# Attention over agents and two feed-forward layers on one core: another issue order at block ends, and three scalings and four additions moved to the pool engine

## Chip, core and metric

One core of a Trainium2 chip. TensorE multiplies matrices into PSUM banks, VectorE and ScalarE read the banks and work on SBUF, the pool engine (POOL in the rows) works on SBUF alone, and SyncE issues DMA transfers. Each engine takes its instructions in program order and waits on semaphores. The metric is the device time of one execution in microseconds (us), lower is better. A time is given as the median of several runs; one further execution was recorded by the profiler.

## What is computed

```
q, k, v: 12480 x 128; agents: 49 x 128; scale = 1 / sqrt(128)
agent_v = softmax(scale * agents @ k.T) @ v              # 49 x 128
x  = softmax(scale * q @ agents.T) @ agent_v             # 12480 x 128
x  = relu(x @ w_in1) ** 2 @ w_out1                       # 128 -> 2048 -> 128
h  = x @ w_in2                                           # 128 -> 2048
out = (max(h, 0) + alpha * min(h, 0)) @ w_out2           # 2048 -> 128
```

All arrays are 32-bit floats or wider on the host.

## The kernel before

A first part, to about 119 us, loads `k`, `v` and the weights and computes the small `agent_v`. It folds `agent_v` into `w_in1` (tiles `W1h`, `W1l`). The main loop then works on the 12480 tokens in 25 blocks, the first of 320 tokens, 23 of 512 and the last of 384. All products are made of three matmuls on a high and a low part of each operand (`...h` and `...l`: a rounded copy and what the rounding left), and each runs as a pair on the two halves of 64 partitions. A "pair" in this text is such two matmuls.

The hidden size of 2048 is cut into eight steps per block (`NP = 8`). Step `s = 8b + i` is step i of block b. One turn of the loop issues, for several blocks at once:

- `H1(s)`, 3 pairs: hidden part of the first layer into bank pair h1, then a relu on ScalarE into `g`. `G1(s)` squares `g` on ScalarE, rounds it on VectorE (`g1h`) and subtracts (`g1l`).
- `O(s - 2)`, 6 pairs: the first layer's output, added up over the eight steps in bank pair o1.
- `H2(s - 11)`, 6 pairs: hidden part of the second layer into bank pair h2; relu on ScalarE into `g2h`, then on VectorE `g2l = max(h, 0) - g2h`.
- `O2`, one step behind its H2, 6 pairs: the second layer's output in bank pair o2. In the first step of a block three more pairs add the linear term: the second layer is written as (1 - alpha) relu(h) + alpha h, and alpha h goes through one 128 x 128 matrix `M` (`Mh`, `Ml`).

h1, h2, o1 and o2 have one buffer each, so a bank pair is filled again only after VectorE and ScalarE have read it. Around the block's end:

- In steps with i = 1 the sums of o1 are complete. `X1(b)` copies one bank on ScalarE, adds the other on VectorE (`x`), makes `xh` on ScalarE and `xl` on VectorE, and issues four DMA copies that exchange the halves of the partitions (`sh`, `sl`). The next block's first O comes at i = 2, the first H2 that reads `xh`, `xl`, `sh` and `sl` at i = 3.
- In the same steps `q_scores` computes the attention scores of the next block (matmuls into h1), and `q_squares` transposes them on VectorE (`s`). At i = 4, ahead of H1, `q_max` runs on VectorE (`mx`, `m`, `s`), at i = 5 `q_norm`.
- The last O2 of a block comes at i = 3. `OUT` copies one bank of o2 on ScalarE and adds the other on VectorE (`o`), transposes (`ot`) and stores; it stands at the head of the turn i = 4, behind `q_max`. The next block's first O2 comes at i = 4.

`M` is built in steps 10 to 19: `m_scale(g)` multiplies a quarter of `w_out2` by alpha (steps 10 to 13; g = 2 on the pool engine, the others on VectorE), `m_join(g)` adds `wi2h` and `wi2l` on VectorE at the end of steps 11, 13, 15 and 17, `m_transpose(g)` turns that on TensorE one step later (bank pair h1, tile `wT_ps`), with a ScalarE copy, and `m_finish(g)` multiplies and adds up two steps later. The order of all this is that of the Python text; no scheduler changes it. In early steps some `g1l` run on the pool engine: `LO_ON_POOL = (0, 3, 4, 6, 7, 9, 10, 11, 15)`.

The engines' work of the loop, as it stands in the turn before the change:

```
            if s < S:
                G1(s)
            bx, ix = divmod(s - LAG1, NP)
            if ix == NP - 1 and 0 <= bx < NB:
                X1(bx)
            if 0 <= s - D < S:
                H2(s - D)
                pend.append(s - D)
```

Of the kernel before, what the change touches and what calls it, by code (L numbers as in the profile page):

```python
# [8 lines left out]
F32 = mybir.dt.float32  # L9
# [3 lines left out]
AF = mybir.ActivationFunctionType  # L13
ALU = mybir.AluOpType
# [5 lines left out]
def agent_attention_moe_kernel(  # L20
# [30 lines left out]
    nc = tc.nc  # L51
# [10 lines left out]
    NP = FC // 2  # L62
    SCALE = 1.0 / float(C) ** 0.5
    QB = 32
    NT = 512
# [4 lines left out]
    NB = len(NQS)  # L70
    H = 64
    GA = (NA + 1) // 2
    LAG1, LAG2 = 2, 1
    D = NP + LAG1 + 1
    S = NB * NP
# [16 lines left out]
    def ps(tag, name):  # L92

        return psum.tile([128, 2, NT], F32, tag=tag, name=name)
# [7 lines left out]
    def rows(r):  # L102
        return slice(r * H, (r + 1) * H)

    def mm2(o, terms, start=True, stop=True):

        for n_, term in enumerate(terms):
            for r in range(2):
                mm(o(r), *term(r), start=(start and n_ == 0), stop=(stop and n_ == len(terms) - 1))

    def f32(ap):
        return ap.bitcast(F32)
# [56 lines left out]
    with tc.manual_schedule():  # L169
# [19 lines left out]
        wi2h = const.tile([128, 2, NP, 128], F32R, name="wi2h")  # L189
        wi2l = const.tile([128, 2, NP, 128], F32R, name="wi2l")  # L190
# [35 lines left out]
        def flat(t_):  # L226
            return t_.rearrange("p j c -> p (j c)")
# [34 lines left out]
        def q_scores(b):  # L262
            if b >= NB:
                return

            n = QB * NQS[b] // 2
            p_ = ps("h1", "s2_ps")[:, :, :n]
            qh, ql = qh_sb.pop(b), ql_sb.pop(b)
            mm2(
                lambda r: p_[:, r],  # L270
                [
                    lambda r, a=a, x=x, h=h: (a[rows(r), h], x[rows(r), h * n:(h + 1) * n])
                    for h in range(2) for a, x in ((agTl, qh), (agTh, ql), (agTh, qh))
                ],
            )
            s2_ps[b] = p_
# [107 lines left out]
        mT = {}  # L384

        def m_scale(g):
            shape = [128, 4, C]
            w4 = aw[g].rearrange("p (k c) -> p k c", c=C)
            (nc.gpsimd if g == 2 else nc.vector).tensor_tensor(
                out=w4, in0=w4, in1=alp[:, 4 * g:4 * g + 4].unsqueeze(2).to_broadcast(shape), op=ALU.mult  # L390
            )

# [2 lines left out]
        def m_join(g):  # L395
            sl = slice(2 * g, 2 * g + 2)
            mT[g] = stg.tile([128, 2, 2, 128], F32, tag="wf", name="wf", bufs=3)
            nc.vector.tensor_tensor(out=mT[g], in0=f32(wi2h[:, :, sl]), in1=f32(wi2l[:, :, sl]), op=ALU.add)

        def m_transpose(g):  # L400
            w = mT[g]
# [26 lines left out]
        with tc.tile_pool(name="att", bufs=1) as att:  # L428
# [191 lines left out]
            for g in range(2):  # L620
                sl = slice(g * NP // 2, (g + 1) * NP // 2)
                p_ = ps(("h1", "h2")[g], "w1_ps")[:, 0].rearrange("p (i m) -> p i m", m=128)
# [7 lines left out]
        xp = ctx.enter_context(tc.tile_pool(name="xp", bufs=2))  # L630

        h1g, h2g, x1, o1p, o2p, outp = {}, {}, {}, {}, {}, {}

        def width(b):
            return QB * NQS[b]

        def H1(s):
            b, i = divmod(s, NP)
            n = width(b)
            p_ = ps("h1", "h1_ps")[:, :, :n]  # L640
            qh, ql = qs_sb[b]
            mm2(
                lambda r: p_[:, r],
                [lambda r, w=w, x=x: (w[rows(r), i], x[rows(r)]) for w, x in ((W1l, qh), (W1h, ql), (W1h, qh))],
            )
            g = wk.tile([128, 2, NT], F32, tag="g1", name="g1")[:, :, :n]
            nc.scalar.activation(g, p_, AF.Relu)  # L647
            h1g[s] = g

        def G1(s):  # L650
            n = width(s // NP)
            g = h1g.pop(s)
            nc.scalar.activation(g, g, AF.Square)  # L653
            gh = wk.tile([128, 2, NT], F32R, tag="g1h", name="g1h", bufs=3)[:, :, :n]
            gl = wk.tile([128, 2, NT], F32R, tag="g1l", name="g1l", bufs=3)[:, :, :n]
            if s in HI_ON_SCALAR:
                nc.scalar.copy(gh, g)  # L657
            else:
                nc.vector.tensor_copy(gh, g)  # L659
            eng = nc.gpsimd if s in LO_ON_POOL else nc.vector  # L660
            eng.tensor_tensor(out=gl, in0=g, in1=f32(gh), op=ALU.subtract)  # L661
            h1g[s] = (gh, gl)

        def O(s, gs, wh, wl, acc, tag):
            b, i = divmod(s, NP)
            if i == 0:
                acc[b] = ps(tag, tag)[:, :, :width(b)]
            p_ = acc[b]
            terms, last = [], []
            if tag == "o2" and i == (NP - 1 if b == 0 else 0):  # L670
                (xh, _), (xl, _) = x1[b]
                (last if b == 0 else terms).extend([lambda r, m=m, x=x: (m[rows(r)], x[rows(r)]) for m, x in ((Ml, xh), (Mh, xl), (Mh, xh))])
            gh, gl = gs.pop(s)
            for j in range(2):
                terms += [
                    lambda r, w=w, g=g, j=j: (w[rows(r), 2 * i + j], g[rows(r), j])
                    for w, g in ((wl, gh), (wh, gl), (wh, gh))
                ]
            mm2(lambda r: p_[:, r], terms + last, start=(i == 0), stop=(i == NP - 1))

        def X1(b):

            p_ = o1p.pop(b)
            n = width(b)
            x = xp.tile([128, NT], F32, tag="x", name="x", bufs=1)[:, :n]
            nc.scalar.copy(x, p_[:, 0])
            nc.vector.tensor_tensor(out=x, in0=x, in1=p_[:, 1], op=ALU.add)  # L687
            xh, sh, xl, sl = (xp.tile([128, NT], F32R, tag=t, name=t)[:, :n] for t in ("xh", "sh", "xl", "sl"))
            nc.scalar.copy(xh, x)  # L689
            nc.vector.tensor_tensor(out=xl, in0=x, in1=f32(xh), op=ALU.subtract)  # L690
            for a, o in ((xh, sh), (xl, sl)):
                for r in range(2):
                    nc.sync.dma_start(out=f32(o[rows(r)]), in_=f32(a[rows(1 - r)]))
            x1[b] = (xh, sh), (xl, sl)
# [19 lines left out]
        def O2(s):  # L714
            O(s, h2g, wo2h, wo2l, o2p, "o2")
            b, i = divmod(s, NP)
            if i == NP - 1:
                x1.pop(b)
                outp[b] = o2p.pop(b)

        def OUT(b):
            p_ = outp.pop(b)
            x = xp.tile([128, NT], F32, tag="o", name="o", bufs=1)[:, :width(b)]
            nc.scalar.copy(x, p_[:, 0])
            nc.vector.tensor_tensor(out=x, in0=x, in1=p_[:, 1], op=ALU.add)  # L725
            ot = xp.tile([128, NT // QB, QB], F32, tag="ot", name="ot")[:, :NQS[b]]
            nc.vector.transpose(flat(ot), x)
            for i in range(C // QB):
                nc.sync.dma_start(out=ov[i][:, Q0[b]:Q0[b] + NQS[b]], in_=ot[i * QB:(i + 1) * QB])
# [14 lines left out]
        for s in range(S + D + 2):  # L744
            b, i = divmod(s, NP)
            if i in before:
                before[i](b + 1)
            for bo in sorted(outp):
                OUT(bo)
            if s < S:  # L750
                H1(s)
            if 0 <= s - LAG1 < S:
                O(s - LAG1, h1g, wo1h, wo1l, o1p, "o1")

            if i == 1:
                q_scores(b + 1)
                q_squares(b + 1)
            for f, t in ((m_transpose, M_STEP + 1), (m_finish, M_STEP + 2)):
                if 0 <= s - t < 8 and (s - t) % 2 == 0:
                    f((s - t) // 2)  # L760
            if s < S:
                G1(s)
            bx, ix = divmod(s - LAG1, NP)
            if ix == NP - 1 and 0 <= bx < NB:
                X1(bx)
            if 0 <= s - D < S:
                H2(s - D)
                pend.append(s - D)
            while pend and len(pend) > (LAG2 if s < S else 2) or pend and s >= S + D:
                O2(pend.pop(0))  # L770
            if i in after:
                after[i](b + 1)
            if i == 0:
                q_load(b + 3)
            at(s_plan, s)
            if 10 <= s < 14:
                m_scale(s - 10)
            if 0 <= s - M_STEP < 8 and (s - M_STEP) % 2 == 0:
                m_join((s - M_STEP) // 2)
# [30 lines left out]
```

## Time and profile before

| what | value |
|---|---|
| median of 3 runs | 1209.27 us (1207.72 to 1211.26) |
| the profiled execution, own time | 1208.35 us |
| its span, first to last instruction | 1206.6 us |
| TensorE busy | 1130.5 us (94%) |
| VectorE busy | 918.8 us (76%) |
| ScalarE busy | 733.2 us (61%) |
| POOL busy | 67.7 us (6%), the last of it at 188 us |
| chain of work that ended last | TensorE 65%, VectorE 20%, ScalarE 8% |

"Busy" of TensorE means that a matmul is recorded as running; matmuls are pipelined and overlap, so the distance between the starts of two pairs says more than the duration of one. "PE" is TensorE's matmuls, "PEld" its weight loads, which run one pair ahead, "DVE" VectorE, "ACT" ScalarE, "SPq" SyncE's DMA queue. A wait is put down to the instruction whose semaphore came last. Line numbers (L711) are those of the kernel before.

### The profile page before, as it was taken

Reading aid. Unit: us, or ns where it says so; the run is one execution under the profiler, and the core shown is the slowest. Engines: PE = TensorE matmul, PEld = TensorE weight load, DVE = VectorE, ACT = ScalarE, POOL = GpSimd, SP = SyncE. Lnnn points to the kernel's source line nnn. Section 1 sums busy time; section 2 is a strip of 40 time slices with the busy share of each in tenths; the row PEclk is TensorE's granted clock in tenths of the full one; section 3 lists DMA queues with packets and bytes.
Section 4 is the critical chain, followed back from the end, with each engine's and each line's share of the span. In section 5 each row is a group of like instructions: output and inputs, shape, how many; then the busy total and the mean of one; then the engine's idle time right before and its main releaser. Section 6 shows DMA issues by size and latency. Waiting matters only on the chain.

```text
span 1206.6 us, 22321 instructions
## 1 busy us (share of the span) xinstructions
PE 1130.5 (94%) x9463; PEld 908.3 (75%) x9463; DVE 918.8 (76%) x1362; ACT 733.2 (61%) x846; POOL 67.7 (6%) x49
## 2 busy tenths in 40 slices
PE   9986678999999999999999999999999999999997
PEld 7985567777777777777777777777777777777786
DVE  3577877887887788788778878878877887887763
ACT  3433655666666666666666666666666666666652
POOL 2136420000000000000000000000000000000000
PEclk9997789999999999999999999999999999999999
DMA  9994101011101111111110111111111011011101
GB/s 216 196 214 103 17 14 27 16 27 27 31 15 36 27 19 27 27 19 27 35 29 12 34 27 18 27 27 22 23 36 27 16 29 25 10 27 23 23 17 23
DMA packets 145283, 48.22 MB, mean 40 GB/s; under 512 B 107101, under 2 KB 138782, under 8 KB 145182
## 3 DMA queue, kind: packets, MB, share of 16 engines
q1 hardware_dynamic: 145182, 46.79, 19.5%
q8 instruction: 74, 1.21, 0.4%
q14 instruction: 27, 0.22, 0.1%
HBM read 27.59 MB, written 6.39 MB: 28 GB/s over the span
## 4 chain that ended last, share of the span: by engine, by line
PE 65%; DVE 20%; ACT 8%; issue 4%; DMA 2%; SPq 0%; DVEq 0%; ACTq 0%
PE o L90 33%; PE h_ps L90 24%; DVE g2l L711 5%; PE s_ps L90 5%; DVE g1h L659 3%; DVE g1l L661 3%; ACT g L653 2%; ACT g L647 2%; ACT g2h L710 2%; PE kT_ps L475 2%; DVE s L292 2%; DVE x L687 1%; DVE o L725 1%; DVE mx L282 1%; ACT xh L689 1%
## 5 line engine op out<-in xcount | busy, mean ns | idle before, releaser
L647 ACT ACTIVATE g<-h_ps 128x1024 f32<-128x1024 f32 (+2 forms) x200 | 200.6, 1003 | 151.5 <-PE h_ps L90 148.5
L710 ACT ACTIVATE g2h<-h_ps 128x1024 fp32r<-128x1024 f32 (+2 forms) x200 | 201.0, 1005 | 141.1 <-PE h_ps L90 125.7
L711 DVE SCALAR_TENSOR_TENSOR g2l<-h_ps,g2h 128x1024 fp32r<-128x1024 f32 (+2 forms) x200 | 238.8, 1194 | 26.4 <-ACT g2h L710 24.7
L659 DVE CAST g1h<-g 128x1024 fp32r<-128x1024 f32 (+2 forms) x198 | 136.4, 689 | 139.3 <-ACT g L653 138.2
L661 DVE TENSOR_TENSOR g1l<-g,g1h 128x1024 fp32r<-128x1024 f32 (+2 forms) x191 | 230.8, 1208 | 7.8 <-ACT g1h L657 1.3
L653 ACT ACTIVATE g<-g 128x1024 f32<-128x1024 f32 (+2 forms) x200 | 207.8, 1039 | 6.2
L90 PE MATMUL o<-g1h,wo1l 64*128 64x512 f32 (+2 forms) x800 | 159.1, 394 | 0.9 <-DVE g1h L659 0.7
L90 PE MATMUL o<-g1l,wo1h 64*128 64x512 f32 (+2 forms) x800 | 157.7, 390 | 1.5 <-POOL g1l L661 1.1
L90 PE MATMUL o<-g1h,wo1h 64*128 64x512 f32 (+2 forms) x800 | 157.4, 390 | 0.0
L90 PE MATMUL o<-g2h,wo2l 64*128 64x512 f32 (+2 forms) x800 | 157.0, 387 | 0.0
L90 PE MATMUL o<-g2l,wo2h 64*128 64x512 f32 (+2 forms) x800 | 156.4, 386 | 0.5 <-DVE g2l L711 0.5
L90 PE MATMUL o<-g2h,wo2h 64*128 64x512 f32 (+2 forms) x800 | 156.2, 386 | 0.0
L90 PE MATMUL h_ps<-xh,wi2l 64*128 64x512 f32 (+2 forms) x400 | 83.2, 412 | 25.6 <-DVE g2l L711 25.6
L90 PEld LDWEIGHTS o<-g1h,wo1l 64*128 64x128 f32 x800 | 76.7, 188 | 22.6 <-DVE x L687 5.7
L90 PEld LDWEIGHTS o<-g1l,wo1h 64*128 64x128 f32 x800 | 76.6, 188 | 18.1 <-POOL g1l L661 2.0
L90 PEld LDWEIGHTS o<-g2l,wo2h 64*128 64x128 f32 x800 | 76.1, 185 | 17.3 <-DVE g2l L711 0.8
L90 PEld LDWEIGHTS o<-g1h,wo1h 64*128 64x128 f32 x800 | 76.5, 187 | 16.3
L90 PEld LDWEIGHTS o<-g2h,wo2h 64*128 64x128 f32 x800 | 76.0, 185 | 16.7
L90 PEld LDWEIGHTS o<-g2h,wo2l 64*128 64x128 f32 x800 | 76.0, 185 | 16.5 <-ACT g2h L710 0.2
L90 PE MATMUL h_ps<-qsh,W1l 64*128 64x512 f32 (+2 forms) x400 | 80.8, 400 | 4.6 <-ACT g L647 2.8
L90 PE MATMUL h_ps<-qsl,W1h 64*128 64x512 f32 (+2 forms) x400 | 79.7, 395 | 0.5 <-DVE qsl L350 0.5
L90 PE MATMUL h_ps<-qsh,W1h 64*128 64x512 f32 (+2 forms) x400 | 79.0, 391 | 0.0
(145 smaller groups left out, 1624.5 us busy)
## 6 DMA issues: line engine op xcount, KB each, us to landing
ring<-in_k_dram SPq DMA_DIRECT2D x13, 480.0 KB, 9.9
ring<-in_v_dram SPq DMA_DIRECT2D x13, 480.0 KB, 9.2
q_sb<-in_q_dram SPq DMA_DIRECT2D x184, 32.0 KB, 1.8
sh<-xh SPq DMA_DIRECT2D x46, 128.0 KB, 2.3
sl<-xl SPq DMA_DIRECT2D x46, 128.0 KB, 2.3
out_dram<-ot SPq DMA_DIRECT2D x92, 64.0 KB, 1.9
raw<-in_moe_w_out_dram SPq DMA_DIRECT2D x8, 512.0 KB, 5.6
raw<-in_moe_w_in_dram SPq DMA_DIRECT2D x4, 512.0 KB, 9.3
```

The costliest lines, as they stand in the source:

```text
L90: nc.tensor.matmul(o, lhsT, rhs, start=start, stop=stop)
L282: nc.vector.tensor_copy(t_[i * QB:(i + 1) * QB, 1, :], t_[o * QB:(o + 1) * QB, 0, :])
L292: nc.vector.transpose(flat(s)[:, r * n:(r + 1) * n], p_[:, r])
L475: nc.tensor.transpose(p_[:, j // TB, (j % TB) * P:(j % TB + 1) * P], t_[:, j, :C], ident[:P, :P])
L647: nc.scalar.activation(g, p_, AF.Relu)
L653: nc.scalar.activation(g, g, AF.Square)
L659: nc.vector.tensor_copy(gh, g)
L661: eng.tensor_tensor(out=gl, in0=g, in1=f32(gh), op=ALU.subtract)
L687: nc.vector.tensor_tensor(out=x, in0=x, in1=p_[:, 1], op=ALU.add)
L689: nc.scalar.copy(xh, x)
L710: nc.scalar.activation(gh, p_, AF.Relu)
L711: nc.vector.scalar_tensor_tensor(out=gl, in0=p_, scalar=0.0, in1=f32(gh), op0=ALU.max, op1=ALU.subtract)
```

## The change

Four edits:

1. X1 is taken apart. Its ScalarE copy (`X1_copy`) is issued behind O, its VectorE addition (`X1_add`) ahead of G1, and the rest (`xh`, `xl` and the DMA copies) behind H2.
2. The square of `g` leaves G1 and is issued right behind O, ahead of `q_scores` and the transposes for `M`.
3. `OUT` is issued behind O2, at the end of the turn, and no longer at the head of the next one.
4. `m_scale` and `m_join` run on the pool engine for every g.

```diff
         def m_scale(g):
-            (nc.gpsimd if g == 2 else nc.vector).tensor_tensor(
+            nc.gpsimd.tensor_tensor(
...
         def m_join(g):
-            nc.vector.tensor_tensor(out=mT[g], in0=f32(wi2h[:, :, sl]), in1=f32(wi2l[:, :, sl]), op=ALU.add)
+            nc.gpsimd.tensor_tensor(out=mT[g], in0=f32(wi2h[:, :, sl]), in1=f32(wi2l[:, :, sl]), op=ALU.add)
...
         def G1(s):
-            nc.scalar.activation(g, g, AF.Square)
...
+        def X1_copy(b):
+            x = xp.tile([128, NT], F32, tag="x", name="x", bufs=1)[:, :width(b)]
+            nc.scalar.copy(x, o1p[b][:, 0])
+            x1[b] = x
+
+        def X1_add(b):
+            nc.vector.tensor_tensor(out=x1[b], in0=x1[b], in1=o1p.pop(b)[:, 1], op=ALU.add)
+
         def X1(b):
-            p_ = o1p.pop(b)
+            x = x1[b]
             n = width(b)
-            x = xp.tile([128, NT], F32, tag="x", name="x", bufs=1)[:, :n]
-            nc.scalar.copy(x, p_[:, 0])
-            nc.vector.tensor_tensor(out=x, in0=x, in1=p_[:, 1], op=ALU.add)
...
             if i in before:
                 before[i](b + 1)
-            for bo in sorted(outp):
-                OUT(bo)
             if s < S:
                 H1(s)
             if 0 <= s - LAG1 < S:
                 O(s - LAG1, h1g, wo1h, wo1l, o1p, "o1")
+            if s < S:
+                nc.scalar.activation(h1g[s], h1g[s], AF.Square)
+            bx, ix = divmod(s - LAG1, NP)
+            ends = ix == NP - 1 and 0 <= bx < NB
+            if ends:
+                X1_copy(bx)
...
+            if ends:
+                X1_add(bx)
             if s < S:
                 G1(s)
-            bx, ix = divmod(s - LAG1, NP)
-            if ix == NP - 1 and 0 <= bx < NB:
-                X1(bx)
             if 0 <= s - D < S:
                 H2(s - D)
                 pend.append(s - D)
+            if ends:
+                X1(bx)
             while pend and len(pend) > (LAG2 if s < S else 2) or pend and s >= S + D:
                 O2(pend.pop(0))
+            for bo in sorted(outp):
+                OUT(bo)
```

How the instructions stand, first on VectorE in a step with i = 1 of the third block (`s_...` is the score tile, `o_1810` the bank of o1). Before:

```order
L292 STREAM_TRANSPOSE s_2304<-s_ps 128x256 x2
L659 CAST g1h<-g_2277 128x1024
L661 TENSOR_TENSOR g1l<-g_2277,g1h 128x1024
L687 TENSOR_TENSOR x<-x,o_1810 128x512
L690 TENSOR_TENSOR xl<-x,xh 128x512
L711 SCALAR_TENSOR_TENSOR g2l<-h_ps,g2h 128x1024
L659 CAST g1h<-g_2361 128x1024
```

and now:

```order
L292 STREAM_TRANSPOSE s_2307<-s_ps 128x256 x2
L686 TENSOR_TENSOR x<-x,o_1810 128x512
L658 CAST g1h<-g_2277 128x1024
L660 TENSOR_TENSOR g1l<-g_2277,g1h 128x1024
L715 SCALAR_TENSOR_TENSOR g2l<-h_ps,g2h 128x1024
L694 TENSOR_TENSOR xl<-x,xh 128x512
L658 CAST g1h<-g_2361 128x1024
```

The addition has moved ahead of `g1h` and `g1l`, and `xl` behind `g2l`. ScalarE in the same step, before:

```order
L647 ACTIVATE g_2277<-h_ps 128x1024
L653 ACTIVATE g_2277<-g_2277 128x1024
L686 COPY x<-o_1810 128x512
L689 CAST xh<-x 128x512
L710 ACTIVATE g2h<-h_ps 128x1024
L647 ACTIVATE g_2361<-h_ps 128x1024
```

and now:

```order
L647 ACTIVATE g_2277<-h_ps 128x1024
L757 ACTIVATE g_2277<-g_2277 128x1024
L682 COPY x<-o_1810 128x512
L714 ACTIVATE g2h<-h_ps 128x1024
L693 CAST xh<-x 128x512
L647 ACTIVATE g_2361<-h_ps 128x1024
```

`xh` and the relu `g2h` have changed places; the square, the copy and the next relu stand as before. The same exchange is made in every block, the last one too.

VectorE two steps later, at the change from i = 3 to i = 4 (`o` is OUT's addition, `mx`, `m` and `s_...` the maximum of the scores). Before:

```order
L711 SCALAR_TENSOR_TENSOR g2l<-h_ps,g2h 128x1024
L300 TENSOR_REDUCE mx<-s_2304 128x16
L282 COPY mx<-mx 32x16 x4
L303 TENSOR_TENSOR m<-mx 128x16
L304 TENSOR_TENSOR s_2304<-s_2304,m 128x16x25
L725 TENSOR_TENSOR o<-o,o_1998 128x512
L727 STREAM_TRANSPOSE ot<-o 128x512
L659 CAST g1h<-g_2490 128x1024
```

and now:

```order
L715 SCALAR_TENSOR_TENSOR g2l<-h_ps,g2h 128x1024
L729 TENSOR_TENSOR o<-o,o_1998 128x512
L731 STREAM_TRANSPOSE ot<-o 128x512
L300 TENSOR_REDUCE mx<-s_2307 128x16
L282 COPY mx<-mx 32x16 x4
L303 TENSOR_TENSOR m<-mx 128x16
L304 TENSOR_TENSOR s_2307<-s_2307,m 128x16x25
L658 CAST g1h<-g_2490 128x1024
```

`o` and `ot` have moved ahead of the maximum; what stands in front of the two and behind them is the same. On ScalarE the copy of OUT has kept its place.

The pool engine from step 9 to its end, where `g_1211`, `g_1273`, `g_1301` and `g_1572` belong to steps 9, 10, 11 and 15, `aw` is a scaling and `wf` a join. Before:

```order
L661 TENSOR_TENSOR g1l<-g_1211,g1h 128x1024
L661 TENSOR_TENSOR g1l<-g_1273,g1h 128x1024
L661 TENSOR_TENSOR g1l<-g_1301,g1h 128x1024
L389 TENSOR_TENSOR aw<-aw,alp 128x512
L661 TENSOR_TENSOR g1l<-g_1572,g1h 128x1024
```

and now:

```order
L660 TENSOR_TENSOR g1l<-g_1211,g1h 128x1024
L660 TENSOR_TENSOR g1l<-g_1273,g1h 128x1024
L389 TENSOR_TENSOR aw<-aw,alp 128x512
L660 TENSOR_TENSOR g1l<-g_1301,g1h 128x1024
L389 TENSOR_TENSOR aw<-aw,alp 128x512
L398 TENSOR_TENSOR wf<-wi2h,wi2l 128x512
L389 TENSOR_TENSOR aw<-aw,alp 128x512 x2
L398 TENSOR_TENSOR wf<-wi2h,wi2l 128x512
L660 TENSOR_TENSOR g1l<-g_1572,g1h 128x1024
L398 TENSOR_TENSOR wf<-wi2h,wi2l 128x512 x2
```

The first join stands behind two scalings and the `g1l` of step 11, the third behind the `g1l` of step 15.

## Rows read from the trace of the kernel before

**Rows 1.** Waits, 215 to 1165 us: who waited for whom, us, times, longest.

```profile
PE h_ps L90 <- DVE g2l L711: 25.6, 22, 1.2
...
PEld o L90 <- DVE x L687: 5.1, 20, 0.3
```

**Rows 2.** Timeline of TensorE: start, duration, engine, operation, [idle before <- releaser].

```profile
543.50 0.40 PE L90 MATMUL o<-g1l,wo1h 64*128 64x512 f32 x2
543.74 0.40 PE L90 MATMUL o<-g1h,wo1h 64*128 64x512 f32 x2
545.32 0.49 PE L90 MATMUL h_ps<-xh,wi2l 64*128 64x512 f32 x2 [1.18 <-DVE g2l L711]
545.65 0.39 PE L90 MATMUL h_ps<-xl,wi2h 64*128 64x512 f32 x2
```

**Rows 3.** Timeline of VectorE, step with i = 1 of the same block.

```profile
539.91 0.65 DVE L659 CAST g1h<-g 128x1024 fp32r<-128x1024 f32 x1
540.60 1.22 DVE L661 TENSOR_TENSOR g1l<-g,g1h 128x1024 fp32r<-128x1024 f32 x1
541.74 0.68 DVE L687 TENSOR_TENSOR x<-x,o 128x512 f32<-128x512 f32 x1
...
544.04 1.22 DVE L711 SCALAR_TENSOR_TENSOR g2l<-h_ps,g2h 128x1024 fp32r<-128x1024 f32 x1 [0.23 <-ACT g2h L710]
```

**Rows 4.** Timeline of ScalarE, same step.

```profile
539.13 0.56 ACT L686 COPY x<-o 128x512 f32<-128x512 f32 x1
...
542.98 1.02 ACT L710 ACTIVATE g2h<-h_ps 128x1024 fp32r<-128x1024 f32 x1
```

**Rows 5.** Timeline, all engines, steps i = 3 to i = 6 of another block.

```profile
294.27 0.69 DVE L659 CAST g1h<-g 128x1024 fp32r<-128x1024 f32 x1 [1.96 <-ACT g L653]
...
299.35 0.39 PE L90 MATMUL h_ps<-sh,wi2h 64*128 64x512 f32 x2
...
300.05 0.51 PE L90 MATMUL o<-xh,Ml 64*128 64x512 f32 x2 [0.32 <-DVE o L725]
...
308.09 1.22 DVE L711 SCALAR_TENSOR_TENSOR g2l<-h_ps,g2h 128x1024 fp32r<-128x1024 f32 x1
...
309.36 0.19 PEld L90 LDWEIGHTS h_ps<-xh,wi2l 64*128 64x128 f32 x2 [0.39 <-DVE g2l L711]
```

**Rows 6.** Timelines of POOL, TensorE and VectorE in steps 10 to 18.

```profile
158.88 2.71 POOL L661 TENSOR_TENSOR g1l<-g,g1h 128x1024 fp32r<-128x1024 f32 x1 [3.16 <-DVE g1h L659]
...
164.54 1.49 POOL L389 TENSOR_TENSOR aw<-aw,alp 128x512 f32<-128x512 f32 x1
...
166.72 0.46 PE L406 MATMUL wT_ps<-ident,wf 64*128 64x64 f32 x8 [3.66 <-DVE wf L398]
...
179.12 0.43 PE L406 MATMUL wT_ps<-ident,wf 64*128 64x64 f32 x7 [1.34 <-DVE wf L398]
...
185.69 2.40 POOL L661 TENSOR_TENSOR g1l<-g,g1h 128x1024 fp32r<-128x1024 f32 x1 [19.66 <-PE h_ps L90]
...
187.19 1.45 DVE L398 TENSOR_TENSOR wf<-wi2h,wi2l 128x512 f32<-128x512 f32 x1
...
202.74 0.47 PE L406 MATMUL wT_ps<-ident,wf 64*128 64x64 f32 x8 [1.14 <-DVE wf L398]
```

**Rows 7.** Waits, 120 to 215 us: TensorE's scores for the query's low part.

```profile
PE s_ps L90 <- DVE ql L260: 2.5, 2, 1.6
```

**Rows 8.** Timelines near the end: ScalarE, SyncE's DMA queue, VectorE, TensorE.

```profile
1174.49 1.03 ACT L710 ACTIVATE g2h<-h_ps 128x1024 fp32r<-128x1024 f32 x1 [0.62 <-PE o L90]
...
1175.10 1.18 SPq L693 DMA_DIRECT2D sl<-xl  x2
...
1175.55 1.23 DVE L711 SCALAR_TENSOR_TENSOR g2l<-h_ps,g2h 128x1024 fp32r<-128x1024 f32 x1 [1.09 <-ACT g2h L710]
...
1177.73 0.58 PE L90 MATMUL h_ps<-sl,wi2h 64*128 64x384 f32 x2
```

**Rows 9.** Tile `sl`: from issue to landing of its 50 transfers.

```profile
DMA to landing us min/median/max: 2.0/2.3/4.3
```

## Prediction

> **What bounds the kernel now.** I read the busy shares first, then who TensorE waits for, then single block ends. TensorE is busy nearly throughout, so the main loop can shorten only where TensorE itself stands still. Write a step as s = 8b + i; i is its place in the block. From 215 to 1165 us TensorE waits 22 times for `g2l`, 25.6 us in all, once per block [rows 1]; its weight loads also wait 20 times for `x`, 0.26 us each. What a wait really costs is read from starts [rows 2]. Pairs of matmuls follow each other every 0.24 us (543.50 to 543.74). Then the first pair of H2 starts 1.58 us later, and the next needs 0.33 us. Against 0.235 each that is 1.35 + 0.10 = 1.45 us lost per block, at H2 of i = 2. This H2 needs the bank pair h2, which VectorE gives back with `g2l` of step i = 1.
>
> Why `g2l` is late is read on two engines. Behind the score transposes VectorE runs `g1h`, `g1l`, the bank addition `x` (to 542.42), then `xl`, which waits for ScalarE's `xh`, and starts `g2l` only at 544.04 [rows 3]. ScalarE has finished the bank copy by 539.69 and starts `g2h` only at 542.98, behind `xh` [rows 4]. So relu and hi/lo of H2 queue behind a conversion that nobody needs for two steps.
>
> **Part 1: X1 taken apart (i = 1).** New VectorE order: transposes, `x`, `g1h`, `g1l`, `g2l`, `xl`. Nothing is added or removed; I lay the durations end to end. `x` may start where `g1h` started, 539.91: the copy has ended at 539.69, 0.22 us earlier [rows 3, 4]. Adding start-to-start distances: `x` to its successor takes about 0.71, `g1h` 0.69 (539.91 to 540.60), `g1l` 1.14 (540.60 to 541.74). That puts `g2l` at 539.91 + 0.71 + 0.69 + 1.14 = 542.45. Its other input, `g2h` (1.02 us), now follows the copy and the end of H2. Counted back from the last O pair at 543.74 [rows 2], with fifteen pairs (O2, H1, O) between, H2's results are there near 540.6, so `g2h` ends near 541.65: VectorE is the later one. `g2l` then ends at 542.45 + 1.22 = 543.67, and 0.05 us later TensorE may go: 543.72. TensorE would want H2 at 543.74 + 0.235, less 0.10 for the `x` wait that also goes (the addition now ends at 540.6, and its bank is wanted at 542.5): 543.88. Its weights would load one pair ahead, at 543.65, so they come 0.07 us late. At i = 6 weights that came 0.35 us late cost only 0.22 us (below), so I take 0.07 as free. Gain per block: 1.45 + 0.10 = 1.55 us, at worst about 1.25 if 0.3 us of wait is left. Over 22 blocks, with the mean wait 1.16 where the block shown has 1.18 [rows 1, 2], that is 22 x 1.52 = **33.4 us**, lower end 27.
>
> What is late next? `xl` now runs behind `g2l` and ends near 544.3; its two copies to the other half of the partitions are issued behind it, 0.6 us apart (1.18 for two [rows 8]). They land 2.3 us after issue, at most 4.3 [rows 9], so the second near 547.3. H2 of i = 3 wants them one step (21 pairs, 4.9 us) and three pairs after 543.88, near 549.4: 2 us to spare. The next `g1h` waits for a square that ends near 544.8, after `xl`. Nothing else moves on this path.
>
> **Part 2: OUT ahead of the maximum (i = 3/4).** The o2 bank now comes free before the four maximum steps, so the wait for `o` goes: 300.05 - 299.35 is 0.70 against 0.235, and 0.11 more in the pair behind it, 0.57 us per block [rows 5]. I count this as **zero**. From `g1h` at 294.27 to `g2l` of i = 5 at 308.09 VectorE runs 27 instructions without an idle entry, and the weights of H2 at i = 6 already wait for that `g2l` (0.39 us, 0.22 lost) [rows 5]. The same instructions between the same two points take the same 15.1 us in another order: H2 of i = 6 still starts 15.1 us after `g1h` of i = 3. The 0.57 moves into the waits at i = 5 and 6. Bounds: 0 to 0.57 x 22 = 12.5 us gain; I take 0 because the idle column is empty.
>
> **Part 3: sums on the pool engine, steps 10 to 18, once.** Three scalings and four joins leave VectorE. POOL's row for the same scaling is 1.49 us (164.54) [rows 6]. In step 12 TensorE stands 3.66 us for the first join, until 166.72. POOL is free at 158.88 + 2.71 = 161.59; before the join now stand a scaling, a `g1l` (2.40 by its row at 185.69) and a scaling: 161.59 + 1.49 + 2.40 + 1.49 + 1.49 = 168.5 instead of 166.6: **+1.9 us** (+1.1 to +3). The third join stands behind `g1l` of step 15: 185.69 + 2.40 + 1.49 = 189.6 instead of 187.19 + 1.45 = 188.6: **+1.0**. The second and fourth joins have an idle POOL, so TensorE's waits of 1.34 and 1.14 us for them go [rows 6], with some 0.15 lost behind each: **-2.8**. Squares ahead of the transposes' copies let VectorE reach `ql` of step 17 earlier, so the smaller of the two waits for `ql` (2.5 in all, the longest 1.6) goes [rows 7]: **-0.9**. Sum **-0.8**, range -3 to +4.
>
> A row speaks against moving work there: VectorE's join at 187.19 took 1.45 us and ended 0.55 us after POOL's `g1l` did (188.09) [rows 6], as if it had stood still until then. The Trainium skill (GPSIMD Engine Reference, Key points) gives the rule: POOL shares its SBUF interfaces with VectorE, and instructions with two SBUF inputs or in a two-port mode contend. By that rule the whole maximum chain of step 12 could crawl between POOL's instructions; this is a rival below.
>
> **Part 4: the tail.** The last X1 sits where ScalarE's `g2h` waits for TensorE until 1174.49 [rows 8]. Before, `xh` and `xl` ran in that idle time. Now `xh` follows that `g2h`, and `xl` follows the `g2l` that ends at 1175.55 + 1.23 = 1176.78. With about 0.55 for its 384 columns, it ends near 1177.3. Before, the first `sl` copy was issued at 1175.10; the second must have gone about 0.6 us later and landed near 1177.8, just when TensorE wants it (1177.73) [rows 8, 9]. Now the second goes near 1177.9 and lands near 1180.0. No other matmul can pass: **+2.2 us** (+1.5 to +3).
>
> **Sum.** Span 1206.6 - 33.4 + 0 - 0.8 + 2.2 = 1174.6. The profiled run's own time is 1.75 above its span, so 1176.35; the median of the three runs is 0.9 above that run: **1177 us**.
>
> **Rivals.**
> Part 2 is real after all. If VectorE's chain could start earlier or has slack that I don't see, 12.5 us more go: 1164.5. For it: the wait for `o` is real. Against it: the empty idle column.
> Only half of part 1. `g2l` is the last link of a VectorE chain with 0.07 us to miss; if the copy came 0.8 us later than 539.69, or the new semaphore waits cost 0.1 to 0.2 us each, 0.75 us per block stays: 1177 + 17 = 1194.
> The first block pays. If POOL's seven instructions in a row (some 12 us) let VectorE pass only one instruction each, the maximum of step 12 ends near 173 and the hi/lo parts behind it hold up two more steps of TensorE; some 2 us each: 1181.
> Slower: the late `xl`. Its transfers now have 2 us where they had nearly 4. From a landing of some 4.4 us on, H2 of i = 3 waits; from some 6 us on, each block loses more than the 1.52 gained; at 6.5 us the time is 1209 + 22 x 0.6 = 1222. The slowest landing of the whole trace is 4.3 us, so this is remote.
> The change doesn't do what it says. If H2 of i = 2 waits for something other than this order, nothing goes and the tail adds 2 us: 1210, within 0.3%. Against it: the row at 544.04 names `g2h` as what `g2l` waited for [rows 3], and `g2h` is what the change moves.
>
> **How the numbers follow.** Forecast 0.70 (1171 to 1184), part 2 real 0.08, half of part 1 0.11, the first block pays 0.07, slower 0.02, no effect 0.02. The range takes the forecast's own spread and the first block's: **1169 to 1186**, which leaves out part 2 in full, the half and the rest, 2 in 10. Faster by over 0.3% (about what a measurement of this kernel can tell from no change) 0.96, within 0.3% 0.02, slower 0.02.
>
> **What would show it.** Part 1: the 22 waits of TensorE for `g2l` fall from 25.6 us to under 4, `x` no longer ends a weight load's wait, and the block's period falls by 1.5 us. Part 2: no wait for `o` within the blocks, but weight loads that wait for `g2l` in two steps per block, some 0.2 and 0.7 us. Part 3: the first wait of `wT_ps` above 5 us, the third near 1, the others gone. Part 4: TensorE waits some 2 us for `sl` near the end. The forecast is wrong if the period falls by less than 0.9 us or by more than 1.9.

## The result

The changed kernel takes 1173.71 us (median of 4 runs, 1171.79 to 1174.41) beside 1209.18 us for the kernel before: a ratio of 0.9703, 95% interval 0.9685 to 0.9721. The forecast was 1177 us within 1169 to 1186. Its profiled execution took 1174.41 us, with a span of 1172.6 us, 34.0 less than before.

| | before | after |
|---|---|---|
| span | 1206.6 us | 1172.6 us |
| TensorE busy | 1130.5 us (94%) | 1116.7 us (95%) |
| VectorE busy | 918.8 us (76%) | 909.4 us (78%) |
| ScalarE busy | 733.2 us (61%) | 737.7 us (63%) |
| POOL busy | 67.7 us | 75.4 us |
| period of a full block | 42.83 us | 41.31 us |

The period is the distance between the starts of the linear term's first pair (`o<-xh,Ml`, i = 4) in successive blocks, as a mean over 19 full blocks in the middle of the loop. It is used below to compare kernels, since kernels with the same loop agree in it closely (to 0.03 us, the last three of the table below to 0.11), while the part up to 119 us differs from one execution to another: its last matmul (`w_ps<-wi,avT`) starts between 116.2 and 119.4 us in the traces.

Set side by side at the same matmuls, the two traces show where the 34 us are. At 118.6 us of before, the end of the first part, they are level (0.08). At 214.6 us the changed kernel is 4.73 us ahead, at 1142.4 us 37.43, at the last matmul 33.95. So the steps before the steady loop gave 4.65, the loop 32.7, and the tail took 3.48 back.

### The profile page after: what moved, and what is told of

Its sections match the earlier page's. It is cut to its first block, busy times and chain, and to the rows that moved or that the text cites. A ratio compares the mean times of both kernels' runs of the same rounds, so it can differ in the third digit from the quotient of the medians.

```text
span 1172.6 us, 22345 instructions
## 1 busy us (share of the span) xinstructions
PE 1116.7 (95%) x9463; PEld 910.2 (78%) x9463; DVE 909.4 (78%) x1355; ACT 737.7 (63%) x846; POOL 75.4 (6%) x56
## 4 chain that ended last, share of the span: by engine, by line
PE 58%; DVE 31%; ACT 5%; issue 2%; POOL 1%; DMA 1%; SPq 0%; DVEq 0%; POOLq 0%
PE o L90 27%; PE h_ps L90 23%; DVE g1l L660 7%; DVE g2l L715 6%; PE s_ps L90 5%; DVE g1h L658 4%; ACT g L647 2%; ACT g L757 2%; PE kT_ps L475 2%; DVE sm L282 2%; DVE mx L282 1%; DVE ot L731 1%; DVE o L729 1%; DVE s L328 1%; DVE s L304 1%
## 5 line engine op out<-in xcount | busy, mean ns | idle before, releaser
L90 PE MATMUL h_ps<-sl,wi2h 64*128 64x512 f32 (+2 forms) x400 | 79.2, 388 | 0.4 <-DMA sl<-xl 0.4
```

The costliest lines, as they stand in the source:

```text
L90: nc.tensor.matmul(o, lhsT, rhs, start=start, stop=stop)
```

## The profile after

Waits of the changed kernel from 215 to 1125 us (who waited for whom, us in total, times, longest), to be read against [rows 1]:

```profile
PEld h_ps L90 <- DVE g2l L715: 23.6, 42, 0.9
PE h_ps L90 <- DVE g2l L715: 8.9, 20, 0.5
```

The row for `x` is gone, and so is any row in which TensorE or its weight loads wait for `o`. The row for `g2l` has fallen from 25.6 to 8.9 us, but not to the 4 that was forecast. A row of a sum doesn't say which waits are in it, so the places are looked up. First VectorE and TensorE around i = 1 and the H2 of i = 2, as in [rows 2, 3] (start, duration, engine, instruction):

```profile
524.63 0.65 DVE L686 TENSOR_TENSOR x<-x,o 128x512 f32<-128x512 f32 x1
525.21 0.68 DVE L658 CAST g1h<-g 128x1024 fp32r<-128x1024 f32 x1
525.92 1.23 DVE L660 TENSOR_TENSOR g1l<-g,g1h 128x1024 fp32r<-128x1024 f32 x1
527.06 1.22 DVE L715 SCALAR_TENSOR_TENSOR g2l<-h_ps,g2h 128x1024 fp32r<-128x1024 f32 x1
528.19 0.68 DVE L694 TENSOR_TENSOR xl<-x,xh 128x512 fp32r<-128x512 f32 x1
```

```profile
528.39 0.40 PE L90 MATMUL o<-g1h,wo1h 64*128 64x512 f32 x2
528.62 0.39 PE L90 MATMUL h_ps<-xh,wi2l 64*128 64x512 f32 x2
528.85 0.40 PE L90 MATMUL h_ps<-xl,wi2h 64*128 64x512 f32 x2
```

VectorE has the forecast order, end to end, and H2 starts 0.23 us behind the last pair of O instead of 1.58 behind it [rows 2]. Nothing is left of that wait. On ScalarE relu and conversion have changed places, as against [rows 4], and VectorE is the later one of the two, as the sum had it:

```profile
525.33 1.03 ACT L714 ACTIVATE g2h<-h_ps 128x1024 fp32r<-128x1024 f32 x1 [0.90 <-PE h_ps L90]
526.25 0.61 ACT L693 CAST xh<-x 128x512 fp32r<-128x512 f32 x1
```

The transfers of `sl`, which now start later, land as fast as before [rows 9]; no H2 of a full block waits for one:

```profile
DMA to landing us min/median/max: 2.0/2.3/3.5
```

Now weight loads and matmuls at H2 of i = 5 (502.67) and i = 6 (508.27) of the block before:

```profile
502.67 0.19 PEld L90 LDWEIGHTS h_ps<-xh,wi2l 64*128 64x128 f32 x2 [0.23 <-DVE g2l L715]
...
508.27 0.19 PEld L90 LDWEIGHTS h_ps<-xh,wi2l 64*128 64x128 f32 x2 [0.88 <-DVE g2l L715]
```

```profile
507.43 0.40 PE L90 MATMUL o<-g1h,wo1h 64*128 64x512 f32 x2
508.27 0.50 PE L90 MATMUL h_ps<-xh,wi2l 64*128 64x512 f32 x2 [0.45 <-DVE g2l L715]
```

and the same two pairs before, at i = 6 of the block of [rows 5]:

```profile
309.01 0.39 PE L90 MATMUL o<-g1h,wo1h 64*128 64x512 f32 x2
309.36 0.50 PE L90 MATMUL h_ps<-xh,wi2l 64*128 64x512 f32 x2
```

Here are the 20 waits. At i = 6 the gap between starts is 0.84; before, its weights came 0.39 us late [rows 5] and the gap was 0.35. It has grown by 0.5 of the 0.57 that the wait for `o` gave free.

## Experiments

Six kernels do or undo one thing, five combine. Ratios are to the kernel before in the same series of runs.

| kernel | median, us | ratio, 95% interval | period, us |
|---|---|---|---|
| X1 taken apart, alone | 1176.16 | 0.9727 (0.9712 to 0.9741) | 41.28 |
| OUT moved, alone | 1206.40 | 0.9995 (0.9980 to 1.0009) | 42.83 |
| sums on POOL, alone | 1207.21 | 0.9993 (0.9981 to 1.0004) | 42.82 |
| square hoisted, alone | 1205.72 | 0.9979 (0.9968 to 0.9989) | 42.82 |
| after, old tail | 1170.51 | 0.9694 (0.9676 to 0.9712) | 41.30 |
| after, `q_norm` behind H2 | 1175.11 | 0.9731 (0.9714 to 0.9747) | 41.26 |
| the same, OUT at its old place | 1183.42 | 0.9803 (0.9786 to 0.9820) | 41.82 |
| `q_norm`, old tail, early joins | 1172.53 | 0.9711 (0.9696 to 0.9727) | 41.25 |
| after, old tail, `q_max` at i = 2 | 1157.20 | 0.9576 (0.9554 to 0.9597) | 40.55 |
| the same, joins ahead of scalings | 1155.88 | 0.9561 (0.9541 to 0.9582) | 40.49 |
| `q_max` at i = 2, sums on VectorE | 1158.14 | 0.9580 (0.9566 to 0.9595) | 40.60 |

### The four parts one by one

**X1 taken apart, alone**, on the kernel before:

```diff
+            if ends:
+                X1_copy(bx)
...
+            if ends:
+                X1_add(bx)
             if s < S:
                 G1(s)
-            if ix == NP - 1 and 0 <= bx < NB:
-                X1(bx)
             if 0 <= s - D < S:
                 H2(s - D)
                 pend.append(s - D)
+            if ends:
+                X1(bx)
```

> The kernel before with X1 taken apart and nothing else. If the gain of the loop comes from this part alone, the period of a block falls from 42.85 us to about 41.3, the 22 waits for g2l at i = 2 shrink to a few hundredths, and the wait for o at i = 4 stays at 0.70 between starts, while weight loads at i = 6 wait as before (0.35 between starts). That is some 34 us less in the loop and 3.5 us more in the tail: about 1179 us. Rival: the period of 41.29 needs OUT's new place as well; then this one keeps part of the loss, with a period of about 41.9 (0.57 more) and some 1192 us.

Measured: 1176.16 us and a period of 41.28, the changed kernel's within 0.03. The rival's 41.9 is out. The waits of this kernel from 215 to 1130 us:

```profile
PEld o L90 <- DVE o L730: 15.0, 21, 0.7
...
PEld h_ps L90 <- DVE g2l L716: 8.2, 21, 0.4
```

No row is left in which a matmul waits for `g2l`. The waits for `o` and the small late weights at i = 6 stand as they stood before, so this one part carries the loop's gain. The time lies 3 us below the 1179 expected; the trace gains 1.3 us ahead of 214.6 us, which the expectation had not counted. The run moves two things at once, the addition ahead of G1 and the conversion to `xh` and `xl` behind H2, and no run separates them. By the durations in [rows 3] the second is nearly all of it: without `xl` in front `g2l` could start when `x` ends, at 542.42, and that is where the sum has it in the new order too (542.45).

**OUT moved, alone**, and nothing else:

```diff
-            for bo in sorted(outp):
-                OUT(bo)
             if s < S:
                 H1(s)
...
                 O2(pend.pop(0))
+            for bo in sorted(outp):
+                OUT(bo)
```

> The kernel before with OUT issued at the end of the turn and nothing else. If VectorE's queue between g1h of i = 3 and g2l of i = 5 sets when H2 of i = 6 may start, the wait for o (0.57 us per block) goes and comes back at i = 6: the period stays at 42.85 within 0.1, the time at 1209 within 2. Rival, OUT's place is worth what its wait costs: period 42.3 and 1197 us.

Measured: no difference (0.9995, the interval holds 1), with the period of before, 42.83. Waits from 215 to 1165 us, and the H2 of i = 6 in one block:

```profile
PE h_ps L90 <- DVE g2l L711: 34.5, 42, 1.2
```

```profile
520.66 0.40 PE L90 MATMUL o<-g1h,wo1h 64*128 64x512 f32 x2
521.51 0.50 PE L90 MATMUL h_ps<-xh,wi2l 64*128 64x512 f32 x2 [0.46 <-DVE g2l L711]
```

No row for `o` is left, but TensorE waits 42 times for `g2l` instead of 22, and 34.5 us instead of 25.6 [rows 1]. The gap at i = 6 is 0.85, the changed kernel's. The wait has moved by two steps, and hardly anything of it has gone.

**Sums on POOL, alone**, and **square hoisted, alone**:

```diff
-            (nc.gpsimd if g == 2 else nc.vector).tensor_tensor(
+            nc.gpsimd.tensor_tensor(
...
-            nc.vector.tensor_tensor(out=mT[g], ...
+            nc.gpsimd.tensor_tensor(out=mT[g], ...
```

> The kernel before with the scalings and joins on the pool engine and nothing else. The prediction's sum for them: first join +1.9, third +1.0, second and fourth -2.8, together about 0, so 1209 within 2. The changed kernel's trace lies 4.3 us ahead of the one before by 200 us. Rival, that this comes from the sums alone, because the first join comes earlier than was worked out: 1205.

```diff
-            nc.scalar.activation(g, g, AF.Square)
...
                 O(s - LAG1, h1g, wo1h, wo1l, o1p, "o1")
+            if s < S:
+                nc.scalar.activation(h1g[s], h1g[s], AF.Square)
```

> The kernel before with the square issued right behind O and nothing else. By the prediction only the wait for ql near 193 us goes: -0.9, and nothing in the later blocks, so 1208 and a period of 42.85. Rival: the square's place is what took 4.3 us from the first 200 us in the changed kernel: 1205.

Measured: the sums make no difference (0.9993, the interval holds 1), so the rival's 1205 is out. The square takes 2.5 us (0.9979, 1.3 to 3.9 us by its interval), which leaves out both the 0.9 of the prediction and the 4.3 of the rival. Between 118.6 and 214.6 us the trace with the sums loses 1.0 us on the kernel before, the one with the square gains 2.5, and X1 alone gains 1.3. Together that is 2.8 of the 4.65. Part of the difference is the granted clock, which changes between its two levels in these steps, and at other places in each trace. From 122 to 129 us it is 0.58 before, 0.76 in the changed kernel and 0.52 in the kernel with the old tail (below), which has the same instructions there; the changed kernel gains 0.8 us in that stretch and the other nothing, and shows 3.75 in all. The trace with the sums has 0.80 from 118.6 to 215 us where before has 0.87, and loses 0.7 us by 122 us and 1.3 at a stretch of 0.50 from 197.4 to 200.8 us, 1.0 of which comes back behind it. So one trace prices a part in these steps to about 1 us, and how the rest divides among the parts stays open. The first join, with the sums alone, then in the changed kernel:

```profile
168.16 0.69 PE L406 MATMUL wT_ps<-ident,wf 64*128 64x64 f32 x8 [4.54 <-POOL wf L398]
```

```profile
165.91 0.51 PE L406 MATMUL wT_ps<-ident,wf 64*128 64x64 f32 x8 [4.53 <-POOL wf L398]
```

With the sums alone the join came at 168.16, 1.44 behind [rows 6]; the forecast said 168.5. But this execution was 0.7 us late at 160 us already: the wait itself is 0.88 longer (4.54 for 3.66), and not 1.9. In the changed kernel, with the square and X1 in their new places, the wait is as long, but it begins and ends 2.25 us sooner; 0.9 of that is the difference that the two executions have at 118.6 us already.

### The tail

The changed kernel with the last block's X1 ahead of H2, as before the change:

```diff
+            if ends and bx == NB - 1:
+                X1(bx)
             if 0 <= s - D < S:
                 H2(s - D)
                 pend.append(s - D)
-            if ends:
+            if ends and bx < NB - 1:
                 X1(bx)
```

> The changed kernel with the last X1 (its xh, xl and copies) ahead of H2 again, as in the kernel before. In the changed kernel TensorE stands some 2.2 us longer at the last block's first H2 for sh and sl, and then works for 3 us at half the granted clock, 1.2 us more. If the half clock comes of the wait, both go: about 1170.2 (3.4 less) and a granted clock of 1.00 throughout the tail. Rival, the clock falls there anyway: 1171.5 (2.2 less).

Measured: 1170.51 us. The two intervals of the ratios overlap, so it is the traces that decide. In the changed kernel the weights of the last block's first H2 wait four times for a transfer:

```profile
1140.49 0.18 PEld L90 LDWEIGHTS h_ps<-sh,wi2l 64*128 64x128 f32 x1 [0.43 <-DMA sh<-xh]
1141.10 0.18 PEld L90 LDWEIGHTS h_ps<-sh,wi2l 64*128 64x128 f32 x1 [0.43 <-DMA sh<-xh]
1141.83 0.18 PEld L90 LDWEIGHTS h_ps<-sl,wi2h 64*128 64x128 f32 x1 [0.54 <-DMA sl<-xl]
1142.42 0.28 PEld L90 LDWEIGHTS h_ps<-sl,wi2h 64*128 64x128 f32 x1 [0.41 <-DMA sl<-xl]
```

Then windows of the changed kernel, of the one with the old tail, and of the one with OUT at its old place (below), which has the same four waits. The columns after the window's length are busy time and count of TensorE, its weight loads, VectorE, ScalarE and POOL, then the granted clock, the DMA share and GB/s:

```profile
1140.00:1142.00 2.00, 1.44 (x7) 0.60 (x5) 1.13 (x1) 0.84 (x1) 0.00 (x0) 1.00 0.61 149
1142.00:1146.00 4.00, 3.85 (x21) 3.59 (x23) 0.10 (x1) 0.00 (x0) 0.00 (x0) 0.57 0.02 4
```

```profile
1139.00:1142.00 3.00, 3.00 (x31) 2.73 (x28) 1.43 (x2) 1.03 (x1) 0.00 (x0) 1.00 0.25 60
1142.00:1146.00 4.00, 4.00 (x41) 3.24 (x37) 1.29 (x3) 1.81 (x3) 0.00 (x0) 1.00 0.02 4
```

```profile
1150.00:1152.00 2.00, 1.39 (x5) 0.55 (x3) 1.23 (x1) 0.53 (x1) 0.00 (x0) 1.00 0.56 137
1152.00:1156.00 4.00, 3.88 (x37) 3.88 (x39) 0.96 (x1) 0.81 (x1) 0.00 (x0) 1.00 0.01 4
```

After its waits the changed kernel has a granted clock of 0.57 for 4 us, most of it at 1.2 instead of 2.4 GHz: 21 matmuls where the old tail has 41. With the old tail neither is there. The kernel in the third pair of rows waits and keeps its full clock. Two more kernels have these waits, X1 alone and `q_norm` behind H2 (below), and in both the clock falls (0.64 and 0.57 over the 4 us behind the waits). That prices the two: from the last full block's linear term to the last block's it is 32.14 us with neither, 34.15 with the wait, 35.68 or 35.69 in the three with the wait and the lower clock. The wait costs 2.0, the clock 1.5.

### What holds the gain of OUT's new place

The changed kernel with `q_norm` (2.6 us on VectorE) moved from the head of i = 5 to the end of that turn, and the same with OUT back at its old place:

```diff
-        before = {..., 4: q_max, 5: q_norm, 6: q_back, 7: q_lo}
-        after = {0: q_split_hi, 4: q_exp, 6: q_hi}
+        before = {..., 4: q_max, 6: q_back, 7: q_lo}
+        after = {0: q_split_hi, 4: q_exp, 5: q_norm, 6: q_hi}
```

> The changed kernel with q_norm (2.6 us on VectorE) behind H2 of i = 5 instead of ahead of H1. What is left of the loop's loss is one gap per block at H2 of i = 6 (0.84 between starts against 0.232, and 0.10 behind it). If VectorE's queue from g1h of i = 3 to g2l of i = 5 is what sets it, the gap goes: 0.7 x 22 = 15.5 us less, period 40.6, about 1158. Rival, the queue only moves on: q_norm and the transposition delay g2l of i = 6, and the gap comes back at H2 of i = 7; period 41.3, 1174.

> As the run with q_norm behind H2 of i = 5, but OUT back at the head of the turn, behind the maximum, as in the kernel before. If OUT's new place was worth nothing only because VectorE's queue gave the gain back at i = 6, it must be worth its 0.57 us per block now that the queue has room: 12.5 us above that run, period 41.2, about 1170. Rival, OUT's place never matters: the same time as that run, 1158.

Measured: the first gains nothing (1175.11 us, period 41.26). The rival named the place: the gap has gone from i = 6 to H2 of i = 7.

```profile
512.76 0.40 PE L90 MATMUL o<-g1h,wo1h 64*128 64x512 f32 x2
513.59 0.50 PE L90 MATMUL h_ps<-xh,wi2l 64*128 64x512 f32 x2 [0.43 <-DVE g2l L715]
```

So the theory was right that VectorE's queue sets it, but it put the queue's end too early: behind `g2l` of i = 5 now come `q_norm`, the transposition, `g1h` and `g1l`, packed against `g2l` of i = 6. What the move did open is an idle entry on VectorE, in front of `g1h` of i = 5. First this kernel, then the one with OUT at its old place:

```profile
504.13 0.69 DVE L658 CAST g1h<-g 128x1024 fp32r<-128x1024 f32 x1 [1.05 <-ACT g L757]
```

```profile
506.48 0.69 DVE L658 CAST g1h<-g 128x1024 fp32r<-128x1024 f32 x1 [1.60 <-ACT g L759]
```

With OUT at its old place, TensorE waits for `o` again (0.66 between starts at i = 4), VectorE then waits for the delayed square 0.55 us longer, and the wait at i = 7 stays (0.89). The period is 41.82, 0.57 above its twin (before rounding): the full price that OUT's place had in the sum of before. The time differs by 8.3 us and not by 12.5. Of the 4.2 missing, 1.6 lie in the tail, where the clock stayed up here, 1.7 ahead of 214.6 us, 1.4 of them in the first part, where both kernels do the same, and 0.7 in the loop. So OUT's place is worth 0.57 us per block where an idle entry lies between it and the next late `g2l`, and nothing where none does.

**`q_max` moved instead.** The idle entry of 1.8 us in front of `g1h` of i = 3 is the one to fill, so the 2.0 us of the maximum go there, to the end of the turn i = 2 (with the old tail kept):

```diff
-        before = {0: q_transpose, 1: q_split_lo, 4: q_max, 5: q_norm, 6: q_back, 7: q_lo}
-        after = {0: q_split_hi, 4: q_exp, 6: q_hi}
+        before = {0: q_transpose, 1: q_split_lo, 5: q_norm, 6: q_back, 7: q_lo}
+        after = {0: q_split_hi, 2: q_max, 4: q_exp, 6: q_hi}
```

> The changed kernel with the last X1 in its old place (3.4 us less, as measured) and q_max (2.0 us on VectorE) at the end of the turn i = 2, ahead of an idle entry of 1.8 us on VectorE, instead of at the head of i = 4, inside the queue without an idle entry. If work that stands between two idle entries of VectorE is what makes g2l late, moving it across the idle entry takes the gap at H2 of i = 6 away for good, and not to i = 7 as with q_norm: period 40.6, 15 us less, about 1155. Rival, H2 of some other step waits instead, as in the run with q_norm: period 41.2 and 1170.

Measured: 1157.20 us, period 40.55. VectorE of this kernel, from the maximum to i = 5:

```profile
488.85 0.58 DVE L304 TENSOR_TENSOR s<-s,m 128x400 f32<-128x400 f32 x1
489.35 0.69 DVE L658 CAST g1h<-g 128x1024 fp32r<-128x1024 f32 x1
...
494.10 0.69 DVE L658 CAST g1h<-g 128x1024 fp32r<-128x1024 f32 x1 [0.33 <-ACT g L757]
...
504.58 0.69 DVE L658 CAST g1h<-g 128x1024 fp32r<-128x1024 f32 x1 [1.18 <-ACT g L757]
```

The maximum runs straight into `g1h` of i = 3, and idle entries stand where there was none. From 215 to 1110 us the waits have no row left in which TensorE or its weight loads wait for VectorE. Against the old tail alone the loop is 15.7 us shorter (15 expected). The whole comes out 2 us above the expected 1155. Ahead of 214.6 us this kernel gives back 2.2, at the first join, where TensorE waits 6.03 instead of 4.54 us and has a granted clock of 0.50 from 164.4 to 171.2 us, where the kernel with the old tail has it from 166.3 to 169.7; the two kernels below with `q_max` in this place lose about 2 us there as well.

### The pool engine's queue

Joins 0 and 1 put into an idle stretch of POOL, step 8, together with `q_norm` behind H2 and the old tail:

```diff
+        SCALES = {10: (0,), 11: (1,), 15: (2, 3)}
+        JOINS = {8: (0, 1), 13: (2,), 15: (3,)}
...
+            for g in SCALES.get(s, ()):
+                m_scale(g)
+            for g in JOINS.get(s, ()):
+                m_join(g)
```

> q_norm behind H2 of i = 5, the last X1 in its old place, and the sums on the pool engine earlier or later: joins 0 and 1 in step 8, where that engine is idle from 147 to 153 us, join 2 in step 13, scalings 2 and 3 and join 3 behind g1l of step 15. TensorE's wait for the first join (4.9 between starts) should go, and with it the half clock behind it (some 1.7): 15.5 + 3.4 + 5 less than the changed kernel, about 1150. Rival, the wait for the first join hides another (the maximum of step 12 and g1l of the same step, which VectorE ends at 170.6): then 2 us of the 5 at most, 1153.

Measured: 1172.53 us. The gain of `q_norm` had fallen already (above). The wait for the first join did go, and yet these steps gave only 2.9 us on the kernel before instead of the changed kernel's 4.65. POOL and VectorE of this kernel, then VectorE of the changed kernel at the same work:

```profile
148.77 3.92 POOL L398 TENSOR_TENSOR wf<-wi2h,wi2l 128x512 f32<-128x512 f32 x2
```

```profile
149.40 2.17 DVE L660 TENSOR_TENSOR g1l<-g,g1h 128x1024 fp32r<-128x1024 f32 x1
151.50 1.74 DVE L260 TENSOR_TENSOR ql<-qT,qh 128x512 fp32r<-128x512 f32 x1
```

```profile
147.69 1.22 DVE L660 TENSOR_TENSOR g1l<-g,g1h 128x1024 fp32r<-128x1024 f32 x1
148.84 0.68 DVE L260 TENSOR_TENSOR ql<-qT,qh 128x512 fp32r<-128x512 f32 x1
```

Beside POOL's two joins, `g1l` and `ql` need 2.0 us more, and TensorE waits 3.6 us for this `ql`. POOL was idle there, but VectorE was not.

The rival came true as well: the wait for the first join had hidden another. The maximum of step 12 still crawls beside POOL, ScalarE's exponential waits 2.68 us for it (at 170.62), and TensorE a little later for the relu behind that:

```profile
165.29 4.48 DVE L282 COPY mx<-mx 32x16 f32<-32x16 f32 x4
```

```profile
172.13 1.16 PE L90 MATMUL M_ps<-aw,wT 128*128 128x128 f32 x8 [2.88 <-ACT g L647]
```

A milder order, with `q_max` at i = 2: join 0 ahead of scaling 1, joins 1 and 2 ahead of the `g1l` of step 15. And the same base with the sums back on VectorE:

```diff
+        SCALES = {10: (0,), 11: (1,), 12: (2,), 13: (3,)}
+        JOINS = {11: (0,), 13: (1, 2), 15: (3,)}
...
+            for g in JOINS.get(s, ())[:1]:
+                m_join(g)
+            for g in SCALES.get(s, ()):
+                m_scale(g)
+            for g in JOINS.get(s, ())[1:]:
+                m_join(g)
```

> As the run with q_max at the end of i = 2, with the pool engine's queue in another order: join 0 ahead of scaling 1, joins 1 and 2 in step 13 ahead of g1l of step 15. The first join ends one scaling (1.0 us) earlier, the third no longer waits behind a g1l of 2.4 us: 1.0 + 0.9 less than that run. Rival, what follows is not ready earlier either (VectorE's own queue of step 12): the same time.

> As the run with q_max at the end of i = 2, with scalings and joins where the kernel before had them, on VectorE except the third scaling. The run with the sums alone on the pool engine made no difference that can be measured, so the same time within 2 us. Rival, with the squares and X1 in their new places VectorE's queue is the one that TensorE waits for in steps 13 to 18, and the sums put joins 2 and 4 back into it: 2 to 3 us more.

Measured: 1155.88 and 1158.14 us beside 1157.20; the intervals overlap, so no time tells the three apart. In the traces the first join's wait is 5.04 instead of 6.03 and the third one's (0.75) is gone, as expected of the milder order. It has the lowest median of all, 0.9561 of the kernel before, and like the other two it is faster than both kernels of the case.

## Why the prediction was right, step by step

**Part 1** held in place and size. Per block the sum had 1.52; the period fell by 1.55 with this part alone, and by 1.52 in the changed kernel. Over the loop it is 33.5 us (X1 alone) against 33.4. The 0.07 us by which the weights were to come late, taken as free, were free: H2 of i = 2 starts at the spacing of any other pair. The rival that keeps half of the loss is out by the period.

**Part 2** held: zero, by the empty idle column. The waits of 0.2 and 0.7 us foretold for the weights at i = 5 and 6 are 0.23 and 0.88. OUT alone measured 0.9995, and the pair of runs with `q_norm` shows that its 0.57 come back as soon as VectorE has an idle entry. One line of "what would show it" was badly put: it wanted the waits for `g2l` below 4 us in the same answer to which part 2 was to send its own waits. They are 8.9 us for that reason.

**Part 3** is the term that was mis-sized: -0.8 forecast within -3 to +4, -4.65 found up to 214.6 us, of which 0.8 goes with the granted clock from 122 to 129 us (above) and not with the change. The sums came to nothing that can be measured, as said, but their terms were off: the wait for the first join grew by 0.88 and not by 1.9, since the second scaling and the join took 1.04 and 1.26 us on POOL (the rows below) where the sum had 1.49 for each, and with the sums alone the gap ahead of the fourth join fell by 0.75 only (1.54 to 0.79 between starts). What failed is the step on the square. It was given only the smaller wait for `ql`, 0.9 us, though it was moved past all four ScalarE copies of `wT`. Alone it also took the gap between starts ahead of the second join from 1.74 us, of which [rows 6] shows 1.34 as a wait, to 0.42, which the sum had credited to the pool engine. And the 22 blocks were counted from 215 us on, while X1 of the second block, at step 17, lies ahead of that: X1 alone gained 0.8 there (between 197.6 and 203.8 us of before).

The rival in which the first block pays came true in its mechanism and not in its price. VectorE's maximum in step 12 of the changed kernel, and POOL beside it:

```profile
161.68 5.21 DVE L282 COPY mx<-mx 32x16 f32<-32x16 f32 x4
166.92 0.96 DVE L303 TENSOR_TENSOR m<-mx 128x16 f32<-128x16 f32 x1
167.92 1.60 DVE L304 TENSOR_TENSOR s<-s,m 128x400 f32<-128x400 f32 x1
```

```profile
161.30 2.34 POOL L660 TENSOR_TENSOR g1l<-g,g1h 128x1024 fp32r<-128x1024 f32 x1
163.60 1.04 POOL L389 TENSOR_TENSOR aw<-aw,alp 128x512 f32<-128x512 f32 x1
164.60 1.26 POOL L398 TENSOR_TENSOR wf<-wi2h,wi2l 128x512 f32<-128x512 f32 x1
165.81 2.04 POOL L389 TENSOR_TENSOR aw<-aw,alp 128x512 f32<-128x512 f32 x2
```

Four copies took 5.21 us, where the four of the next step, with POOL idle, took 0.71 (at 172.18): one copy passed for each instruction of POOL. The maximum ended at 169.5, not at 173. TensorE stood waiting for the join until 165.91 anyway and was busy without a break from 167 to 173 us, so it cost nothing that can be seen here. Where the wait for the join was taken away (the run with early joins), it did cost 2.9.

**Part 4**: the wait was sized rightly, 2.0 us for 2.2 said. The tail cost 3.5 us because the granted clock fell behind the wait, 1.5 us that the sum did not have. In one of the four kernels with that wait it did not fall, so the 1.5 are not certain in every execution. The trace of before had shown the like, a granted clock of 0.72 from 167 to 173 us behind the wait for the first join, and the prediction left it out.

Of the 3.3 us between 1177 and 1173.7, the span has 2.0: 3.9 more gained in part 3, 1.3 more lost in the tail, 0.7 less gained in the loop. The rest is the median, which lay 0.9 above the profiled run before and lies 0.7 below it now. So the time came this near by a sound part 1, which is nearly the whole change, and by some luck in the small terms: part 3 and the tail missed in opposite directions.

## What to carry to other kernels

Before a wait is counted as a gain, look down the idle column of the engine that ends it, to the next place where the waiting engine needs that engine: without an idle entry between, the wait only moves. To get the gain, take work across an idle entry (the maximum to i = 2: 15.7 us), not along inside the packed stretch (`q_norm`: 0). And a place where POOL is idle is free only if VectorE is idle there too, or works on what POOL doesn't hold up.

## What the runs showed of the hardware

- Beside POOL instructions, VectorE's small copies from SBUF to SBUF stood still for most of an instruction each (5.21 against 0.71 us for four), and two-input instructions took about 1 us longer (`ql` 1.74 against 0.68, the maximum's subtraction 1.60 against 0.58), while `g2l`, which reads PSUM and one SBUF tile, kept its time (0.81 us at 160.36, with a scaling of POOL beside it). The Trainium skill (SBUF — State Buffer, Terms) describes a pair of ports that the two engines share as taken exclusively and held for a whole instruction, so that the other engine blocks. The trace agrees: each of the four copies ends 0.03 us behind an instruction of POOL.
- Four waits of 0.4 to 0.5 us within 2.5 us were followed by 4 us at a granted clock of 0.57 in the changed kernel, 0.64 with X1 alone and 0.57 with `q_norm` behind H2 (TensorE busy 1.44, 1.41 and 1.34 of 2 us in the waits), and by none of that in a fourth kernel with the same waits (1.39 of 2 us). What decided between them no run here shows.
